# Float32 attention scores on 64 array rows per head for the first 14 head pairs, each loaded by fewer transfers

## The chip, the cores and the metric

One core of a Trainium2 chip runs the kernel. The metric is device time in microseconds of one execution, lower is better. Names of engines: PE is TensorE's matmul, PEld its weight load, DVE VectorE, ACT ScalarE, POOL GpSimd, SP the engine that issues most transfers.

## The reference

```python
batch, n_heads, seq, head_dim = (8, 12, 448, 64)

def _attn_ref(q, k, v):
    S = q.shape[2]
    scale = 1.0 / np.sqrt(q.shape[-1])
    scores = scale * np.matmul(q, k.transpose(0, 1, 3, 2)) - np.log(S)
    attn = 1.0 / (1.0 + np.exp(-scores))
    return np.matmul(attn, v).astype(np.float32)

def _moe_ref(x, w_in, w_out):          # x (3584, 768), w_in (768, 2048), w_out (2048, 768)
    h = x @ w_in
    beta = 1.0
    neg = h <= -beta
    pos = h >= beta
    g = np.where(pos, h, np.where(neg, 0.0, (h + beta) ** 2 / (4.0 * beta)))
    return (g @ w_out).astype(np.float32)
```

Attention weights are sigmoids, not a softmax. The attention output of all heads is laid out as 3584 tokens by 768 and goes through the feed-forward part. All inputs are float32; the weights come as 64-bit words whose two halves the kernel turns into float32 itself.

## The kernel before

*Pairs and pieces.* Two heads of 64 dimensions make one pair, so a batch has 6 pairs (`NP`) and there are 48 in all. A pair is worked in four pieces of keys (`NPC`): three of 128 keys and one "half piece" of the last 64, whose two heads share one tile. For each piece PE computes the scores of both heads (`scores`, tile `psc`, two buffers), ACT the sigmoid (`weigh`, lines 387 and 390), and PE multiplies it with v (`av`, line 436, tile `pav`). After the last piece the result is copied to `x32` (line 442 or 445). Pieces are counted through: piece 4p + c is the piece c of pair p.

*Three ways to compute scores.* Pairs 0 to 5 (`NFULL`) stay in float32. Their k is loaded twice over, each head's half beside zeros, so that a matmul over all 128 rows gives one head (line 339):

```python
out = psc[j * D : (j + 1) * D, 0, :S] if mid else psc[:, j, :S]
nc.tensor.matmul(out, r[:, 2 + j, w], r[:, 0, :], start=True, stop=True)
```

Pairs 6 to 13 (`NHALF`) have q and k scaled and split into a high and a low float16 part: the largest value by DVE (`prep_a`, line 275), a sum over partitions by PE (line 129), scales (line 106 on) and the split by ACT and DVE (`prep_b`, lines 310 and 311), then eight small transfers on SP that place the parts for stacked matmuls (lines 320 and 321, tile `qk`). A full piece is then two matmuls on 128 rows (line 346) and two on 64 rows (line 355), one per head each. Their v and attention weights stay float32. Pairs 14 to 47 split v and the weights too (lines 341, 361, 403, 404).

*Feed-forward.* The weights come in 16 chunks of 768 KB each for w_in and w_out. A chunk is loaded (line 166), converted by ACT (line 185) and DVE (lines 194, 195), its maximum taken (line 209, or 211 on ACT for w_out), and, once eight chunks have given a common scale, split to two float16 parts (lines 228, 229). `finish_x` scales and splits a batch's `x32` into `xhl` (lines 465, 466). `up` gives `ph` (line 534, 18 matmuls a chunk) and the activation `g` (lines 543 to 547), `down` gives `po` (line 566). The tiles `ph`, `po` and those of the small maxima share three buffers.

*Order of the work.* `step(i)` puts in the scores that run ahead and the `av` of piece i, and at given pieces the loads and preparations of later pairs. While batch b goes through `up` and `down`, the attention of batch b + 1 is dealt out between their units. The loads on SP keep program order in the opening; so does PE from batch 2 on. Everything else in batches 0 and 1 (PE, ACT, DVE, and SP later) is ordered by a list scheduler that plans with its own estimates of time, so an edit to one step can move others. Each engine then works through its list in that order, and waits where an operand isn't there yet. In the opening the loads of pairs 0 to 7 and of w_in are issued interleaved:

```python
load_pair(0)
wi.load(1, nc.sync)
load_pair(1)
wi.load(2, nc.sync)
load_pair(2)
wi.load(3, nc.sync)
```

and each conversion of a w_in chunk issues the load of a later one into the place that it freed (line 201).

Of the kernel before, what the change touches and what calls it, by code (L numbers as in the profile page):

```python
# [23 lines left out]
P = 128  # L24
# [9 lines left out]

NFULL = 6
NHALF = 8

# [11 lines left out]
L0 = 10  # L49
A0 = 17  # L50
LSTEP = 1
# [5 lines left out]
def sigmoid_attention_mlp(ctx: ExitStack, tc: tile.TileContext, first_qvk, qkv, w_in, w_out, out_t):  # L57
    nc = tc.nc
    NFULL, _, _, S = first_qvk.shape
    B = out_t.shape[1] // S  # L60
# [188 lines left out]
    def load_pair(p):  # L249
        if p >= NPAIR or not first_time("load", p):  # L250
            return
        if p < NFULL:
            r = full[:, p % NFB]
            nc.sync.dma_start(out=r[:D, 2, :], in_=first_qvk[p, :D, 2, :])
            nc.sync.dma_start(out=r[D:, 3, :], in_=first_qvk[p, D:, 2, :])
            nc.sync.dma_start(out=r[:, 0:2, :], in_=first_qvk[p, :, 0:2, :])
            ready[p] = r, r[:, 1]
            return
        src = qkv[p - NFULL]
        raws[p] = raw_p.tile([P, 2 * S + VW], F32, tag="raw", name="raw")  # L260
        if p < NFULL + NHALF:
            v = stk_p.tile([P, VW], F32, tag="v", name="v", bufs=3)
            nc.sync.dma_start(out=raws[p][:, : 2 * S], in_=src[:, : 2 * S])
            nc.sync.dma_start(out=v, in_=src[:, 2 * S :])
            ready[p] = v
        else:
            nc.sync.dma_start(out=raws[p], in_=src)

    def prep_a(p, total=True):
        if NFULL <= p < NPAIR and first_time("max", p):  # L270
            n = 2 if p < NFULL + NHALF else 3
            m = sml_p.tile([P, 3], F32, tag="m3", name="m3", bufs=2)
            parts = [(m[:, 0:2], raws[p][:, : 2 * S].rearrange("p (t n) -> p t n", t=2)), (m[:, 2:3], raws[p][:, 2 * S :])]
            for mt, rt in parts[: n - 1]:
# [13 lines left out]
    def prep_b(p):  # L288
        if not NFULL <= p < NPAIR or not first_time("split", p):
            return  # L290
        add_up(p)
        r, m = raws.pop(p), maxes.pop(p)[1]
        n = 2 if p < NFULL + NHALF else 3

# [5 lines left out]
        hl = stk_p.tile([P, 2, 2, S], F16, tag="hl", name="hl")  # L300
        parts = [hl[:, 0], hl[:, 1]]
        if n == 3:
            v = stk_p.tile([P, 2, VW], F16, tag="v", name="v", bufs=3)
            parts.append(v)
        else:
            v = ready[p]
        for t, dst in enumerate(parts):
# [18 lines left out]
    def scores(todo):  # L326

        tiles = []
        for i in todo:
            p, c = divmod(i, NPC)  # L330
            mid = c == NKC
            w = slice(c * P, S if mid else (c + 1) * P)
            psc = ps_sc.tile([P, 2, 512], F32, tag="psc", name="psc")
            tiles.append(psc)
            if p < NFULL:
                r = ready[p][0]
                for j in range(2):
                    out = psc[j * D : (j + 1) * D, 0, :S] if mid else psc[:, j, :S]
                    nc.tensor.matmul(out, r[:, 2 + j, w], r[:, 0, :], start=True, stop=True)  # L339
            elif mid and p >= NFULL + NHALF:  # L340
                nc.tensor.matmul(psc[:, 0, :S], corner(p), ready[p][4][:, 0, 1, :], start=True, stop=False)
            else:
                kq = ready[p][0]
                for j in range(2):
                    out = psc[j * D : (j + 1) * D, 0, :S] if mid else psc[:, j, :S]
                    nc.tensor.matmul(out, kq[:, j, 1, w], kq[:, j, 0, :], start=True, stop=False)  # L346
        for i, psc in zip(todo, tiles):
            p, c = divmod(i, NPC)
            mid = c == NKC
            if p >= NFULL and not (mid and p >= NFULL + NHALF):  # L350
                hl, w = ready[p][4], slice(c * P, S if mid else (c + 1) * P)
                for j in range(2):
                    rows = slice(j * D, (j + 1) * D)
                    out = psc[rows, 0, :S] if mid else psc[:, j, :S]
                    nc.tensor.matmul(out, hl[rows, 1, 0, w], hl[rows, 0, 1, :], start=False, stop=True)  # L355
        for i, psc in zip(todo, tiles):
            p, c = divmod(i, NPC)
            if p >= NFULL + NHALF and c == NKC:
                kq = ready[p][0]
# [6 lines left out]
        for p, c in (divmod(i, NPC) for i in todo):  # L366
            if c == 0 and p >= NFULL + NHALF:
                if p < NFULL + NHALF + 2:
                    nc.gpsimd.memset(corner(p), 0.0)
# [8 lines left out]
    def weigh(i, psc):  # L378
# [4 lines left out]
        a = psc[:, :n, :S]  # L383
        sqk = 1.0 / math.sqrt(D) if p < NFULL else ready[p][2]
        if p < NFULL + NHALF:
            a32 = att_p.tile([P, 2, S], F32, tag="ahl", name="a32")
# [22 lines left out]
    def av(i):  # L409
# [9 lines left out]
        v = ready[p][1]  # L419
        split = p >= NFULL + NHALF  # L420
        terms = []
        for j in range(2):
            o = slice(j * D, (j + 1) * D)
            full_v = slice((2 * c + j) * D, (2 * c + j + 1) * D)
            if p < NFULL and mid:
                full_v = slice(2 * c * D, (2 * c + 1) * D)
# [13 lines left out]
        if mid:  # L440
            if p < NFULL + NHALF:
                nc.scalar.activation(x32[:, hp, :], pav[:, :S], AF.Copy)
# [186 lines left out]
    with tc.manual_schedule(engines={mybir.EngineType.SP}):  # L629
# [9 lines left out]
        while at < NPIECE:  # L639
            step(at)  # L640
            at += 1
            for what, when in ((load_pair, L0), (prep_a, A0), (prep_b, A0 + 1)):
                for k in range(2):
                    if at == when + LSTEP * k:
                        what(NFULL + k)
            convert(wi, min((NA + 1) * at // WI_A, NA + 1 + max(0, at - WI_A) * (NFC - NA) // (NPIECE - WI_A + WI_B)))
# [110 lines left out]
```

## Time and profile before

| | us |
|---|---|
| median of 3 runs | 1175.96 |
| lowest and highest | 1175.06, 1177.38 |
| the profiled execution | 1175.71 |
| its span, first to last instruction | 1174.0 |

The span is what the trace covers; the rest of an execution's time lies around it. The page gives for each engine its busy time, which for PE is near to the span; busy PE can still be PE at work on matmuls that are slower than they need be, so the timeline's steps from one start to the next say more than the durations. A float32 matmul leaves two records in the trace, a float16 matmul one. In the timeline the numbers behind a tile's name are the array's rows and columns that the matmul uses. PEclk is the granted clock, where 1.00 is 2.4 GHz and 0.50 is 1.2 GHz.

### The profile page before, as it was taken

Reading aid. Unit: us, or ns where it says so; the run is one execution under the profiler, and the core shown is the slowest. Engines: PE = TensorE matmul, PEld = TensorE weight load, DVE = VectorE, ACT = ScalarE, POOL = GpSimd, SP = SyncE. Lnnn points to the kernel's source line nnn. Section 1 sums busy time; section 2 is a strip of 40 time slices with the busy share of each in tenths; the row PEclk is TensorE's granted clock in tenths of the full one; section 3 lists DMA queues with packets and bytes.
Section 4 is the critical chain, followed back from the end, with each engine's and each line's share of the span. In section 5 each row is a group of like instructions: output and inputs, shape, how many; then the busy total and the mean of one; then the engine's idle time right before and its main releaser. Section 6 shows DMA issues by size and latency. Waiting matters only on the chain.

```text
span 1174.0 us, 16804 instructions
## 1 busy us (share of the span) xinstructions
PE 1154.9 (98%) x6368; PEld 556.7 (47%) x6368; DVE 792.9 (68%) x1576; ACT 620.3 (53%) x897; POOL 30.5 (3%) x76
## 2 busy tenths in 40 slices
PE   7999999999999999999999999999999999999998
PEld 2334444454455444554455445454444544455554
DVE  6899986867644886578864887568865788326510
ACT  5788875644433665456643775446563557404300
POOL 0000000000000000000000000000000000000000
PEclk9989999999999999999999999999999999999999
DMA  9758352142112113111212221212123111000000
GB/s 328 276 183 287 104 166 93 43 134 65 49 56 65 41 41 97 57 56 44 78 58 65 59 72 49 72 54 77 41 60 94 56 42 25 24 25 8 1 16 32
DMA packets 49233, 93.71 MB, mean 80 GB/s; under 512 B 7936, under 2 KB 37888, under 8 KB 49152
## 3 DMA queue, kind: packets, MB, share of 16 engines
q1 hardware_dynamic: 47424, 83.20, 22.8%
q10 hardware_dynamic: 1728, 9.44, 2.3%
q8 instruction: 50, 0.82, 0.3%
q14 instruction: 31, 0.25, 0.1%
HBM read 60.95 MB, written 12.39 MB: 62 GB/s over the span
## 4 chain that ended last, share of the span: by engine, by line
PE 66%; DVE 17%; ACT 7%; DMA 7%; issue 2%; SPq 1%; ACTq 0%; DVEq 0%
PE po L566 37%; PE ph L534 16%; PE pav L436 6%; DMA raw<-qkv 5%; PE psc L346 3%; DVE g L545 2%; PE psc L339 2%; DVE m L275 2%; DVE g L544 2%; PE psc L355 2%; DVE ahl L404 2%; DVE ghl L547 2%; ACT psc L390 2%; ACT ghl L546 1%; DVE xhl L466 1%
## 5 line engine op out<-in xcount | busy, mean ns | idle before, releaser
L534 PE MATMUL ph<-xhl,w_in_sb 128*128 128x448 f16 x2304 | 448.7, 354 | 5.6 <-ACT xhl L465 2.7
L566 PE MATMUL po<-ghl,w_out_sb 128*128 128x448 f16 x2304 | 444.2, 353 | 0.0
L534 PEld LDWEIGHTS <-w_in_sb 128*128 128x128 f16 x2304 | 222.2, 98 | 225.0 <-issue 25.2
L566 PEld LDWEIGHTS <-w_out_sb 128*128 128x128 f16 x2304 | 222.0, 98 | 217.7 <-issue 13.4
L390 ACT ACTIVATE psc<-psc,nls,sqk 128x896 f32<-128x896 f32 (+1 forms) x136 | 126.8, 967 | 94.2 <-PE psc L355 93.3
L404 DVE SCALAR_TENSOR_TENSOR ahl<-psc,ahl 128x896 f16<-128x896 f32 x102 | 109.0, 1084 | 36.0 <-ACT ahl L403 35.7
L546 ACT ACTIVATE ghl<-g 128x448 f16<-128x448 f32 x128 | 73.6, 575 | 112.8 <-DVE g L545 111.4
L547 DVE TENSOR_TENSOR ghl<-g,ghl 128x448 f16<-128x448 f32 x128 | 79.6, 622 | 51.1 <-ACT ghl L546 50.9
L543 ACT ACTIVATE g<-ph,hr,ihr 128x448 f32<-128x448 f32 x128 | 91.7, 723 | 34.6 <-PE ph L534 30.1
L275 DVE TENSOR_REDUCE m<-raw 128x2 f32<-128x896 f32 x76 | 66.1, 902 | 53.5 <-DMA raw<-qkv 53.3
L576 DVE TENSOR_SCALAR o<-po,od 128x448 f32<-128x448 f32 x48 | 32.6, 681 | 90.9 <-PE po L566 82.0
L403 ACT ACTIVATE ahl<-psc 128x896 f16<-128x896 f32 x102 | 90.2, 913 | 0.0
L545 DVE SCALAR_TENSOR_TENSOR g<-ph,ihs,g 128x448 f32<-128x448 f32 x128 | 86.9, 681 | 2.5
L310 ACT ACTIVATE hl<-raw,qkv_s 128x448 f16<-128x448 f32 x84 | 51.7, 663 | 66.8 <-DVE qkv_i L112 50.7
L544 DVE SCALAR_TENSOR_TENSOR g<-g,rk 128x448 f32<-128x448 f32 x112 | 75.9, 680 | 15.2 <-ACT g L543 13.1
L346 PE MATMUL psc<-qk 128*128 128x448 f16 (+1 forms) x268 | 67.0, 354 | 1.7 <-DMA qk<-hl 1.6
L465 ACT ACTIVATE xhl<-x,x_s 128x448 f16<-128x448 f32 x48 | 27.7, 659 | 77.4 <-DVE x_s L108 77.4
L436 PE MATMUL pav<-ahl,v 128*64 128x448 f16 x612 | 64.2, 353 | 0.0
L311 DVE SCALAR_TENSOR_TENSOR hl<-raw,qkv_s,hl 128x448 f16<-128x448 f32 x84 | 54.8, 680 | 7.7 <-ACT hl L310 7.1
L436 PEld LDWEIGHTS <-v 128*64 128x64 f16 x748 | 42.3, 110 | 26.5 <-issue 0.9
L372 POOL COPY w_in_sb<-hl 64x64 f16<-64x64 f16 x68 | 29.4, 432 | 831.7 <-ACT hl L310 811.0
L339 PE MATMUL psc<-ghl 128*128 128x448 f32 (+1 forms) x96 | 39.2, 587 | 6.1 <-DMA ghl<-first_qvk 5.9
(109 smaller groups left out, 783.9 us busy)
## 6 DMA issues: line engine op xcount, KB each, us to landing
raw<-qkv SPq DMA_DIRECT2D x34, 704.0 KB, 4.4
qk<-hl SPq DMA_DIRECT2D x336, 56.0 KB, 2.0
w_out_sb<-w_in SPq DMA_DIRECT2D x16, 768.0 KB, 9.8
out_t<-o SPq DMA_DIRECT2D x48, 224.0 KB, 1.9
w_out_sb<-w_out ACTq DMA_DIRECT2D x6, 768.0 KB, 4.6
raww<-w_out ACTq DMA_DIRECT2D x6, 768.0 KB, 6.0
raw<-qkv SPq DMA_DIRECT2D x8, 448.0 KB, 6.2
w_out_sb<-w_out SPq DMA_DIRECT2D x4, 768.0 KB, 8.4
```

The lines of the kernel that those rows point to most:

```text
L275: nc.vector.tensor_reduce(out=mt, in_=rt, axis=AX.X, op=ALU.max, apply_absolute_value=True)
L346: nc.tensor.matmul(out, kq[:, j, 1, w], kq[:, j, 0, :], start=True, stop=False)
L390: nc.scalar.activation(a, a, AF.Sigmoid, bias=nls, scale=sqk)
L403: nc.scalar.activation(hi, x, AF.Copy, scale=ATT)
L404: nc.vector.scalar_tensor_tensor(out=lo, in0=x, scalar=ATT, in1=hi, op0=ALU.mult, op1=ALU.subtract)
L436: nc.tensor.matmul(pav[j * D : (j + 1) * D, :S], *terms[j][t], start=c == 0 and t == 0, stop=mid and t == len(terms[j]) - 1,)
L534: nc.tensor.matmul(ph[:, :S], w_in_sb[:, f, wh, c * P : (c + 1) * P], xhl[:, c, xh, :], start=c == 0 and wh + xh == 0, stop=c == NCC - 1 a ...
L543: nc.scalar.activation(g, ph[:, :S], AF.Relu, bias=hr, scale=ihr)
L544: nc.vector.scalar_tensor_tensor(out=g, in0=g, scalar=rt, in1=g, op0=ALU.min, op1=ALU.mult)
L545: nc.vector.scalar_tensor_tensor(out=g, in0=ph[:, :S], scalar=ihs, in1=g, op0=ALU.mult, op1=ALU.max)
L547: (nc.gpsimd if f % GPOOL else nc.vector).tensor_tensor(out=ghl[:, f, 1, :], in0=g, in1=hi, op=ALU.subtract)
L566: nc.tensor.matmul(po[:, :S], w_out_sb[:, f, wh, m * P : (m + 1) * P], ghl[:, f, gh, :], start=f == lo and wh + gh == 0, stop=f == hi - 1 ...
```

## The change

Pairs 0 to 13 (`NF32`) now take one path. Scores are one float32 matmul per head on the 64 rows that hold the head's q and k: head 0 on rows 0 to 63, head 1 on rows 64 to 127, with both heads issued one after the other. k is no longer doubled and no zeros are set. For pairs 0 to 5 (`NFIRST`) q, k and v lie side by side in memory and come in one transfer (pair 0: q and k, then v), into five buffers instead of four. Pairs 6 to 13 keep their two transfers, but their q and k are used as loaded: the maximum, the sum, the split and the eight small transfers are gone for them. Pairs from 14 on are as before. The order in which `load_pair` and `wi.load` are called is as before.

```diff
-NFULL = 6
-NHALF = 8
+NFIRST = 6
+NF32 = 14
...
-    NFB = 4
-    full = ghl.rearrange("p f h n -> p (f h n)").bitcast(F32).rearrange("p (b t n) -> p b t n", b=NFB, t=4)
-    for i in range(NFB):
-        nc.vector.memset(full[D:, i, 2, :], 0.0)
-        nc.vector.memset(full[:D, i, 3, :], 0.0)
+    NFB = 5
+    full = ghl.rearrange("p f h n -> p (f h n)")[:, : NFB * 6 * S].bitcast(F32)
+    full = full.rearrange("p (b t n) -> p b t n", b=NFB, t=3)
...
-        if p < NFULL:
+        if p < NFIRST:
             r = full[:, p % NFB]
-            nc.sync.dma_start(out=r[:D, 2, :], in_=first_qvk[p, :D, 2, :])
-            nc.sync.dma_start(out=r[D:, 3, :], in_=first_qvk[p, D:, 2, :])
-            nc.sync.dma_start(out=r[:, 0:2, :], in_=first_qvk[p, :, 0:2, :])
-            ready[p] = r, r[:, 1]
+            for t in (slice(0, 2), slice(2, 3)) if p == 0 else (slice(0, 3),):
+                nc.sync.dma_start(out=r[:, t, :], in_=first_qvk[p, :, t, :])
+            ready[p] = (r[:, 0], r[:, 1]), r[:, 2]
             return
...
-        if p < NFULL + NHALF:
+        raw = raw_p.tile([P, 2 * S + VW], F32, tag="raw", name="raw")
+        if p < NF32:
             v = stk_p.tile([P, VW], F32, tag="v", name="v", bufs=3)
-            nc.sync.dma_start(out=raws[p][:, : 2 * S], in_=src[:, : 2 * S])
+            nc.sync.dma_start(out=raw[:, : 2 * S], in_=src[:, : 2 * S])
             nc.sync.dma_start(out=v, in_=src[:, 2 * S :])
-            ready[p] = v
+            ready[p] = (raw[:, :S], raw[:, S : 2 * S]), v
...
-            if p < NFULL:
-                r = ready[p][0]
+            if p < NF32:
+                q, k = ready[p][0]
                 for j in range(2):
-                    out = psc[j * D : (j + 1) * D, 0, :S] if mid else psc[:, j, :S]
-                    nc.tensor.matmul(out, r[:, 2 + j, w], r[:, 0, :], start=True, stop=True)
+                    rows = slice(j * D, (j + 1) * D)
+                    out = psc[rows, 0, :S] if mid else psc[:, j, :S]
+                    nc.tensor.matmul(out, k[rows, w], q[rows, :], start=True, stop=True)
```

Elsewhere `NFULL + NHALF` becomes `NF32`, the preparations of the split run from pair 14 on only, and the host packs q, k, v of pairs 0 to 5 in this order.

The scheduler deals the work out anew. Two places:

ACT in the opening, before: conversions of w_in chunks 7 to 10 (line 185) among the sigmoids (line 387, `a` is the sigmoid's tile), in full, piece 10 to 15, and the first split (line 228).

```order
L387 ACTIVATE a_220<-psc,nls 128x896 [waits PE_49,Activation_49]
L387 ACTIVATE a_237<-psc,nls 128x448 [waits PE_49,Activation_49]
L185 ACTIVATE w_in_sb<-w_out_sb 128x768 [waits DMAHW6_49]
L185 ACTIVATE w_in_sb<-w_out_sb 128x768 [waits DMAHW7_49]
L387 ACTIVATE a_245<-psc,nls 128x896 [waits PE_49,Activation_49]
L185 ACTIVATE w_in_sb<-w_out_sb 128x768 [waits DMAHW0_49]
L387 ACTIVATE a_261<-psc,nls 128x896 [waits PE_49,Activation_49]
L442 ACTIVATE x_91<-pav 128x448 [waits PE_49]
L387 ACTIVATE a_277<-psc,nls 128x896 [waits PE_49,Activation_49]
L387 ACTIVATE a_286<-psc,nls 128x448 [waits PE_49,Activation_49]
L185 ACTIVATE w_in_sb<-w_out_sb 128x768 [waits DMAHW6_49]
L228 ACTIVATE w_in_sb<-w_in_sb,wi_s 128x768 [waits DVE_49]
```

ACT now, the same four conversions (now line 184): they stand among pieces 6 to 9 (line 379).

```order
L434 ACTIVATE x_91<-pav 128x448 [waits PE_49]
L184 ACTIVATE w_in_sb<-w_out_sb 128x768 [waits DMAHW5_49]
L379 ACTIVATE a_157<-psc,nls 128x896 [waits PE_49,Activation_49]
L184 ACTIVATE w_in_sb<-w_out_sb 128x768 [waits DMAHW6_49]
L379 ACTIVATE a_171<-psc,nls 128x448 [waits PE_49,Activation_49]
L184 ACTIVATE w_in_sb<-w_out_sb 128x768 [waits DMAHW7_49]
L379 ACTIVATE a_184<-psc,nls 128x896 [waits PE_49,Activation_49]
L379 ACTIVATE a_191<-psc,nls 128x896 [waits PE_49,Activation_49]
L184 ACTIVATE w_in_sb<-w_out_sb 128x768 [waits DMAHW3_49]
L434 ACTIVATE x_91<-pav 128x448 [waits PE_49]
L227 ACTIVATE w_in_sb<-w_in_sb,wi_s 128x768 [waits DVE_49]
L379 ACTIVATE a_203<-psc,nls 128x896 [waits PE_49,Activation_49]
```

Chunk 10's conversion stood behind the sigmoids of 16 pieces and now stands behind those of 10; chunks 2 to 15 all moved up in this way against the sigmoids.

PE while the attention of batch 1 runs among the feed-forward of batch 0, before: the third piece of pair 11, its four matmuls in one row.

```order
L346 MATMUL psc_1479<-qk_1222 128x448 [waits Activation_49]
L346 LDWEIGHTS qk_1222
L346 MATMUL psc_1479<-qk_1222 128x448
L355 LDWEIGHTS hl_1217
L355 MATMUL psc_1479<-hl_1217 128x448
L355 LDWEIGHTS hl_1217
L355 MATMUL psc_1479<-hl_1217 128x448
L566 LDWEIGHTS w_out_sb_90 [waits DVE_49]
```

PE now, the same piece (line 333), between `po` matmuls (line 558):

```order
L558 LDWEIGHTS w_out_sb_90
L558 MATMUL po_1183<-ghl_93,w_out_sb_90 128x448
L333 MATMUL psc_1213<-raw_791 128x448 [waits PE_49]
L558 LDWEIGHTS w_out_sb_90 [waits DVE_49]
L558 MATMUL po_1183<-ghl_93,w_out_sb_90 128x448
L333 MATMUL psc_1213<-raw_791 128x448
L558 LDWEIGHTS w_out_sb_90 [waits Activation_49]
```

The two heads' matmuls of this piece now have a `po` matmul between them. In the whole list this is so for four score pieces: three full ones (the first of pairs 8 and 12, and this one) and the half piece of pair 11. The `pav` pairs that are torn in this way are two now and were four before.

## Rows read from the trace of the kernel before

**Rows 1.** The page: its first line, and PE's part of its first section.
```profile
span 1174.0 us, 16804 instructions
PE 1154.9 (98%) x6368; PEld 556.7 (47%) x6368; DVE 792.9 (68%) x1576; ACT 620.3 (53%) x897; POOL 30.5 (3%) x76
```

**Rows 2.** PE's list of waits: who waited for whom, us in total, times, longest us.
```profile
PE ph L534 <- ACT xhl L465: 2.7, 1, 2.7
PE psc L346 <- DMA qk<-hl: 1.6, 3, 1.0
```

**Rows 3.** PE's timeline, opening: start us, us, engine, line, operation, records, idle before.
```profile
27.51 1.77 PE L339 MATMUL psc<-ghl 128*128 128x448 f32 x4
29.21 0.97 PE L436 MATMUL pav<-a,ghl 64*64 64x448 f32 x4
30.11 2.67 PE L339 MATMUL psc<-ghl 128*128 128x448 f32 x8
32.61 1.67 PE L436 MATMUL pav<-a,ghl 128*64 128x448 f32 x8
34.22 1.77 PE L339 MATMUL psc<-ghl 128*128 128x448 f32 x4
```

**Rows 4.** PE's timeline, pairs 5 to 7 and the first `ph`.
```profile
62.25 0.55 PE L346 MATMUL psc<-qk 128*128 128x448 f16 x2
62.73 0.36 PE L355 MATMUL psc<-hl 64*128 64x448 f16 x2
63.02 0.97 PE L436 MATMUL pav<-a,ghl 128*64 128x448 f32 x4
...
64.71 0.97 PE L436 MATMUL pav<-a,ghl 64*64 64x448 f32 x4
65.61 0.55 PE L346 MATMUL psc<-qk 128*128 128x448 f16 x2
...
66.39 0.38 PE L346 MATMUL psc<-qk 128*64 128x448 f16 x2
...
67.00 1.72 PE L436 MATMUL pav<-a,v 128*64 128x448 f32 x8
...
76.25 0.53 PE L534 MATMUL ph<-xhl,w_in_sb 128*128 128x448 f16 x1 [2.71 <-ACT xhl L465]
...
76.65 12.80 PE L534 MATMUL ph<-xhl,w_in_sb 128*128 128x448 f16 x53
```

**Rows 5.** Windows: busy of PE, PEld, DVE, ACT, POOL; PEclk, DMA share, GB/s.
```profile
15.00:20.00 5.00, 5.00 (x18) 1.65 (x16) 3.94 (x6) 3.21 (x4) 0.00 (x0) 1.00 1.02 418
2.60:41.30 38.70, 35.23 (x111) 12.87 (x113) 26.90 (x40) 23.44 (x29) 0.00 (x0) 1.00 1.02 367
75.40:82.00 6.60, 5.75 (x17) 2.39 (x17) 6.60 (x18) 6.45 (x12) 0.00 (x0) 0.50 0.15 60
```

**Rows 6.** SP's timeline, then the list of DMA issues (KB, us to landing): w_in chunk 10.
```profile
31.61 0.36 SPq L166 DMA_DIRECT2D w_out_sb<-w_in  x1
...
w_out_sb<-w_in SPq DMA_DIRECT2D x1, 768.0 KB, 9.7
```

**Rows 7.** ACT's timeline from the end of pair 3's third full piece on.
```profile
48.05 1.01 ACT L387 ACTIVATE a<-psc,nls 128x896 f32<-128x896 f32 x1 [1.59 <-PE psc L339]
48.96 0.54 ACT L442 ACTIVATE x<-pav 128x448 f32<-128x448 f32 x1
49.38 0.90 ACT L185 ACTIVATE w_in_sb<-w_out_sb 128x768 f32<-128x768 f32 x1
50.17 0.94 ACT L228 ACTIVATE w_in_sb<-w_in_sb,wi_s 128x768 f16<-128x768 f32 x1
51.00 1.54 ACT L387 ACTIVATE a<-psc,nls 128x896 f32<-128x896 f32 x2
```

**Rows 8.** PE's timeline, later: one head of `pav` alone.
```profile
162.33 0.96 PE L436 MATMUL pav<-a,v 64*64 64x448 f32 x2
163.22 0.55 PE L346 MATMUL psc<-qk 128*128 128x448 f16 x2
```

More of the change, by code (lines that the diff above doesn't have):

```diff
@@ L49 @@
 L0 = 10
-A0 = 17
 LSTEP = 1
@@ L288, in prep_b @@
     def prep_b(p):
-        if not NFULL <= p < NPAIR or not first_time("split", p):
+        if not NF32 <= p < NPAIR or not first_time("split", p):
             return
@@ L300, in prep_b @@
         hl = stk_p.tile([P, 2, 2, S], F16, tag="hl", name="hl")
[L301 to L306, printed above, removed]
+        v = stk_p.tile([P, 2, VW], F16, tag="v", name="v", bufs=3)
+        parts = [hl[:, 0], hl[:, 1], v]
         for t, dst in enumerate(parts):
@@ L344, in scores @@
                 for j in range(2):
-                    out = psc[j * D : (j + 1) * D, 0, :S] if mid else psc[:, j, :S]
-                    nc.tensor.matmul(out, kq[:, j, 1, w], kq[:, j, 0, :], start=True, stop=False)
+                    nc.tensor.matmul(psc[:, j, :S], kq[:, j, 1, w], kq[:, j, 0, :], start=True, stop=False)
         for i, psc in zip(todo, tiles):
@@ L349, in scores @@
             mid = c == NKC
-            if p >= NFULL and not (mid and p >= NFULL + NHALF):
-                hl, w = ready[p][4], slice(c * P, S if mid else (c + 1) * P)
+            if p >= NF32 and not mid:
+                hl, w = ready[p][4], slice(c * P, (c + 1) * P)
                 for j in range(2):
                     rows = slice(j * D, (j + 1) * D)
-                    out = psc[rows, 0, :S] if mid else psc[:, j, :S]
-                    nc.tensor.matmul(out, hl[rows, 1, 0, w], hl[rows, 0, 1, :], start=False, stop=True)
+                    nc.tensor.matmul(psc[:, j, :S], hl[rows, 1, 0, w], hl[rows, 0, 1, :], start=False, stop=True)
         for i, psc in zip(todo, tiles):
             p, c = divmod(i, NPC)
-            if p >= NFULL + NHALF and c == NKC:
+            if p >= NF32 and c == NKC:
                 kq = ready[p][0]
@@ L366, in scores @@
         for p, c in (divmod(i, NPC) for i in todo):
-            if c == 0 and p >= NFULL + NHALF:
-                if p < NFULL + NHALF + 2:
+            if c == 0 and p >= NF32:
+                if p < NF32 + 2:
                     nc.gpsimd.memset(corner(p), 0.0)
@@ L419, in av @@
         v = ready[p][1]
-        split = p >= NFULL + NHALF
+        split = p >= NF32
         terms = []
@@ L424, in av @@
             full_v = slice((2 * c + j) * D, (2 * c + j + 1) * D)
-            if p < NFULL and mid:
+            if p < NFIRST and mid:
                 full_v = slice(2 * c * D, (2 * c + 1) * D)
@@ L589, in step @@
         p, c = divmod(i, NPC)
-        early = p >= NFULL + NHALF
+        early = p >= NF32
         if c == 0:
@@ L596, in step @@
                 prep_a(p + 2)
-        if c == 1 and p >= NFULL + NHALF - 1:
+        if c == 1 and p >= NF32 - 1:
             prep_a(p + 3, False)
@@ L600, in step @@
             prep_b(p + 2)
-        if c == 3 and p >= NFULL + NHALF - 2:
+        if c == 3 and p >= NF32 - 2:
             load_pair(p + 4)
         if not early:
-            more, some = i + LAG + 1 + (p == NFULL + NHALF - 1 and c == NKC), [i]
+            more, some = i + LAG + 1 + (p == NF32 - 1 and c == NKC), [i]
         else:
@@ L641, in sigmoid_attention_mlp @@
             at += 1
[L642 to L645, printed above, removed]
+            for k in range(2):
+                if at == L0 + LSTEP * k:
+                    load_pair(NFIRST + k)
             convert(wi, min((NA + 1) * at // WI_A, NA + 1 + max(0, at - WI_A) * (NFC - NA) // (NPIECE - WI_A + WI_B)))
@@ L739 @@
     half = vp[:, :, NK * P :]
-    n = NFULL
-    first = np.stack([qt[:n], np.concatenate([whole[:n], half[:n].reshape(n, P, D)], 2), kt[:n]], 2)
+    n = NFIRST
+    first = np.stack([qt[:n], kt[:n], np.concatenate([whole[:n], half[:n].reshape(n, P, D)], 2)], 2)
     half = half[n:].transpose(0, 2, 1, 3).reshape(B * NP - n, P // 2, P)
```

24 lines of the change are left out of this document (12 added, 12 removed).

## Prediction

> **What bounds the kernel now.** I read the page first. PE is busy 1154.9 of 1174.0 us [rows 1], so a change pays only if it takes work off PE or closes one of PE's few gaps. The list of PE's waits names those gaps in the part that changes: 2.7 us in one piece before the first `ph`, which waits for `xhl`, and 1.6 us in three pieces where scores wait for the small loads of `qk` [rows 2].
>
> Then PE's timeline of the opening, where pairs 0 to 5 run in float32 [rows 3]. A piece is up to 128 keys of one pair, with both heads; each pair has three full pieces and one half piece (keys 384 to 447). A float32 matmul leaves two records. From start to start, the scores of a full piece take 1.70 us (27.51 to 29.21), because the two heads use all 128 rows one after the other. The two heads of `pav` share the array by columns and take 0.90 us. A full and a half piece together take 2.50 us, so the half piece, whose heads lie side by side, takes 0.80; two `pav` in a row take 1.61.
>
> Rows 4 show pairs 6 and 7, which use split float16. A full piece takes 0.77 us (62.25 to 63.02) and a half piece 0.61 (66.39 to 67.00). The last `pav` of batch 0 ends at 65.61 and the first `ph` starts at 76.25. I call the first of these T. After the gap the granted clock stands at 0.50, that is 1.2 GHz, from 75.4 to 82.0 us; PE is busy 5.75 us of that stretch [rows 5] and half of it, 2.9 us, is lost.
>
> Last, the loads. From 2.6 to 41.3 us the 16 DMA engines are fully busy and move 367 GB/s; in a stretch where most of what moves is weights it is 418 [rows 5]. The eleventh w_in chunk (number 10) is issued at 31.61 and lands 9.7 us later, at 41.3 [rows 6].
>
> **The change, part by part.**
>
> *Scores of pairs 0 to 5.* Eighteen full pieces lose one of their two passes over the array. The trace has no float32 matmul on 64 rows by 128 columns. Nearest is the float32 pair on 64 rows by 64 columns, 0.90 us for both heads (64.71 to 65.61) [rows 4]; the lower bound is the half piece's 0.80, the upper the 1.70 of two heads in turn [rows 3]. I take 0.88. In float16 the form 64 by 128 is there: both heads take 0.29 us (62.73 to 63.02) [rows 4], against 0.48 for the two full-array matmuls before them, so they do overlap. With `pav` a pair then costs 3 x 0.88 + 0.80 + 3.4 = 6.8 us, 1.71 a piece, where it cost 9.31 (1.70 + 0.90 + 2.50 + 1.61 + 1.70 + 0.90). PE saves some 13 us in the opening.
>
> A rule speaks against the half pieces, whose two heads write one PSUM bank. The Trainium skill, TensorEngine Tiling (Array Packing), Restrictions and Gotchas, says that different row tiles cannot access the same bank at once. By that rule each half piece would take about 1.7 us, not 0.88. The trace does not bear it out: the `pav` half pieces on 64 by 64 write one bank with both heads and take 0.90.
>
> *Does the saving reach T?* I think not, and this is the centre of the forecast. ACT works in order, and the scheduler has placed the w_in conversions much earlier: chunk 10 now stands after ten sigmoids, before it stood after sixteen. But chunk 10 comes behind the same 13.5 MB (eleven chunks of 0.79 MB, pairs 0 to 6), and the engines are already full. The pair loads become one block of 5.4 KB a row instead of rows of 1.8 and 3.6 KB; if pairs move at 418 instead of some 335 GB/s, six pairs of 0.69 MB gain 2.4 us. So chunk 10 lands at about 38.9 (bounds 36.4, everything at 418, and 41.3, as now), and ACT holds the next sigmoid, PE the next scores, until then. PE idles some 5 us.
>
> From there I count ACT by start-to-start times [rows 7]: conversion 0.79, `x` copy 0.42, split 0.83, sigmoid 0.91 gives 41.85. Up to the sigmoid of piece 16 stand four full sigmoids and two half ones (0.50), five conversions (chunks 11 to 15), four splits and one copy: 3.6 + 1.0 + 4.0 + 3.3 + 0.4 = 12.3 us, ending at 54.2. PE needs 6 x 1.71 = 10.3 for the same pieces, so ACT sets the pace, and PE has 2.0 us of slack. A gap of 2.7 us was enough to halve the clock [rows 2, 5]; after a gap of 5 I charge 2.9 again, of which 0.9 is not covered. Then PE sets the pace with 8 scores and 8 `pav`, 13.7 us. T = 54.2 + 13.7 + 0.9 = 68.8, which is 3.2 us **later** than the 65.6 of before.
>
> *From T to the first `ph`.* The order has four scores and four `pav` there, 6.85 us: `ph` starts at 75.65. The chain to `xhl` fits in this (copy, maximum, transpose, scales, first xhl, some 5 us when DVE is not holding pair preparation), so the 2.7 us wait and the slow clock after it go. Before, two more score pieces were done by then: 1.75 us. Front: (75.65 + 1.75) - (76.25 + 2.9) = **-1.75**, bounds -4.2 and +0.6 from the landing.
>
> *Scores of pairs 8 to 13, beside the feed-forward work.* PE is full here, so work counts fully. A pair cost 3 x 0.77 + 0.61 = 2.92; it now costs 4 x 0.88 = 3.5. Six pairs: **+3.5**, bounds +1.7 (0.80 a piece) and +5.2 (0.95).
>
> *Torn pieces.* In the new PE order four score pieces have `ph` or `po` matmuls between their heads. A lone float32 head takes 0.89 (162.33 to 163.22) [rows 8], as much as a pair. Torn scores add 4 x 0.85; torn `pav` pairs fall from four to two. Net **+1.7**.
>
> *What is dropped.* Eight maxima, sixteen splits on ACT and on DVE, 64 small `qk` loads on SP, eight fills of zeros on DVE at the start. Of all this PE waits only for the `qk` loads: **-1.6** [rows 2]. The rest is freed time on engines that PE doesn't wait for.
>
> *What is added in waits.* Raw q and k now stay in use until the scores have read them. On SP the load of pair 8 waits for the scores of pair 6, at T + 1.7, and w_out chunks 0 and 1 are queued behind it. Chunk 2 waits behind the load of v of pair 9, which waits for pair 6's last `pav` (75.65). ACT converts these in order, ahead of the `g` that frees `ph`'s buffers: with some 7 us for chunk 2's load (9.7 in a full stretch [rows 6]) and two more operations, the first `g` comes at about 85. PE needs the buffer after three `ph` and two pieces, some 13 us after its start, at 89 (53 `ph` matmuls took 12.8 us at mostly half clock [rows 4]; I take 10 for 54). The margin is thin, so I charge **+1.5**, between 0 and 5, a little over the 4.3 us of waits that PE has there now [rows 2].
>
> *Sum.* -1.75 + 3.5 + 1.7 - 1.6 + 1.5 = +3.35. The profiled execution took 1175.71 us, 0.25 under the median of the runs, 1175.96. That gives **1179.0 us**.
>
> **Rivals.**
>
> 1. *ACT is not held, and the opening runs at PE's new pace.* PE would need only 1.71 us a piece, ACT some 42 us in all (18 x 0.91 + 6 x 0.50 + 16 x 0.79 + 9 x 0.83 + 6 x 0.42). If the chunks landed early enough for T = 60, the front would gain 8.8 more: 1170. It decides at T = 65.4, where the sum is zero. For it: DVE drops the pair preparation, and SP issues fewer and larger loads. Against it: even for 65.4 chunk 10 would have to land at 35.5, that is 13.5 MB in 33 us, 410 GB/s for everything, against 367 in the same stretch now [rows 5]. Chance 0.22.
> 2. *No change that can be measured.* The landing at its early bound, a piece at 0.82, no new wait: 3.35 - 2.5 - 1.4 - 1.5, a little faster; any one of them alone gives 1176.5 to 1178. Chance 0.27.
> 3. *The heads do not overlap.* Full pieces alone: eleven on the way to `ph` that ACT doesn't cover and fifteen later that aren't torn anyway, times 0.82, 21 us: 1200. Against it stand the pairs at 0.29 and 0.90 [rows 4]. If the heads of the half pieces took turns, the twelve on the way or later would cost 0.85 more each, 10 us: 1189. The rule of the Trainium skill, TensorEngine Tiling (Array Packing), that is cited above would have it so; the 0.90 speaks against it. Chance of either 0.05.
> 4. *A longer hold of ACT by w_out loads*: each load that ACT awaits with a score's sigmoid behind it costs up to 5 us; 1182 to 1188. It is in the upper part of my range.
>
> **How the numbers follow.** The smallest change a measurement of this kernel tells is about 0.2%, 2.35 us. The forecast and rival 4 hold 0.46, rival 3 has 0.05: slower 0.51. Rival 2: 0.27. Rival 1: 0.22. The likeliest case alone spans 1175 to 1188. The range of 8 in 10 goes down to rival 1's 1170, and up to 1188, where late landing (+2.4), 0.95 a piece (+1.7) and 5 us of waits (+3.5) together give 1186.6.
>
> **What would show it.** Scores of a full piece in the opening near 0.88 from start to start, both heads starting together; 1.7 would be rival 3. ACT waiting for w_in loads between 20 and 40 us where now it waits for PE; a PE gap of 4 to 5 us ended by a sigmoid near 41; a second stretch at half clock there. T between 66 and 71, `ph` starting at 73 to 78 with no wait for `xhl`. No wait of scores for `qk`. After 82 us, a little more score time and four torn pieces. If T is below 64, the centre of this forecast is wrong; if T is right but the end is not, the terms after `ph` are.

## The result and the profile after

The changed kernel takes **1184.24 us** (median of 4 runs, 1183.12 to 1185.78), the kernel before, beside it, 1176.63. The ratio of the runs is 1.0071, with a 95% interval of 1.0056 to 1.0087: slower. The medians differ by 7.6 us (their own quotient is 1.0065). The forecast was 1179, slower, with 1170 to 1188. The profiled execution of the changed kernel is the longest of its four, 1185.78 us, 10.1 above that of before; the accounts below are between these two executions.

The page's first lines stand against [rows 1]: PE is as busy as before in a span that is 10.1 us longer, so PE has lost time to waiting: it is idle in 29.6 us of the span, before in 19.1. Within its busy time a gain and a loss cancel: the scores of the opening got cheaper and later ones dearer, so that all score matmuls together take 148.3 us from start to start, before 149.3.

```profile
span 1184.1 us, 16533 instructions
PE 1154.5 (97%) x6360; PEld 548.6 (46%) x6360; DVE 769.9 (65%) x1496; ACT 609.8 (51%) x881; POOL 30.2 (3%) x76
```

PE's list of waits, changed kernel (who waited for whom, us in all, times, longest). Both entries of [rows 2] are gone, and a new one heads the list: scores (line 333) that wait for the sigmoid (line 379) to free their buffer, which was 0.2 us before.

```profile
PE psc L333 <- ACT a L379: 13.1, 7, 5.1
PE psc L333 <- DMA ghl<-first_qvk: 4.1, 1, 4.1
PE pav L428 <- ACT x L434: 3.6, 4, 2.2
PE ph L526 <- DVE g L537: 3.2, 5, 1.5
PE psc L335 <- DVE ahl L396: 1.6, 4, 0.5
```

PE's timeline of the opening. A full piece's scores take 0.95 us from start to start (18.64 to 19.59), where [rows 3] had 1.70: the heads do overlap. But PE stands still three times in the opening, 5.14, 4.06 and 2.19 us. The last `pav` of batch 0 ends at 70.59 (before: 65.6), the first `ph` starts at 77.96 (before: 76.25), without a wait for xhl and at full clock.

```profile
12.59 1.86 PE L333 MATMUL psc<-ghl 64*128 64x448 f32 x4 [5.14 <-ACT a L379]
...
18.64 1.02 PE L333 MATMUL psc<-ghl 64*128 64x448 f32 x4
19.59 0.97 PE L428 MATMUL pav<-a,ghl 128*64 128x448 f32 x4
...
27.43 1.34 PE L333 MATMUL psc<-ghl 64*64 64x448 f32 x4 [4.06 <-ACT a L379]
...
39.60 1.72 PE L428 MATMUL pav<-a,ghl 128*64 128x448 f32 x8 [2.19 <-ACT x L434]
...
69.69 0.97 PE L428 MATMUL pav<-a,ghl 64*64 64x448 f32 x4
70.59 1.92 PE L333 MATMUL psc<-raw 64*128 64x448 f32 x8
...
77.96 10.39 PE L526 MATMUL ph<-xhl,w_in_sb 128*128 128x448 f16 x54
```

ACT's timeline tells what each sigmoid stood behind: w_in conversions (line 184) that wait for their loads. The row at 38.23 is chunk 10, which had its place behind ten pieces' sigmoids. The three stops of PE end right behind the rows at 9.33 (with the table load and the sigmoid after it), 25.58 and 38.23.

```profile
9.33 0.89 ACT L184 ACTIVATE w_in_sb<-w_out_sb 128x768 f32<-128x768 f32 x1 [7.25 <-DMA w_out_sb<-w_in]
...
25.58 0.89 ACT L184 ACTIVATE w_in_sb<-w_out_sb 128x768 f32<-128x768 f32 x1 [2.61 <-DMA w_out_sb<-w_in]
26.38 0.99 ACT L379 ACTIVATE a<-psc,nls 128x896 f32<-128x896 f32 x1
...
29.10 0.90 ACT L184 ACTIVATE w_in_sb<-w_out_sb 128x768 f32<-128x768 f32 x1 [1.29 <-DMA w_out_sb<-w_in]
...
38.23 0.89 ACT L184 ACTIVATE w_in_sb<-w_out_sb 128x768 f32<-128x768 f32 x1 [2.61 <-DMA w_out_sb<-w_in]
39.02 0.53 ACT L434 ACTIVATE x<-pav 128x448 f32<-128x448 f32 x1
```

Later, a torn score piece between `po` matmuls (PE's timeline): each head takes 0.95 us (168.34 to 169.29) by itself, as long as both side by side.

```profile
168.34 1.02 PE L333 MATMUL psc<-raw 64*128 64x448 f32 x2
169.29 0.36 PE L558 MATMUL po<-ghl,w_out_sb 128*128 128x448 f16 x1
169.59 1.02 PE L333 MATMUL psc<-raw 64*128 64x448 f32 x2
170.53 0.55 PE L558 MATMUL po<-ghl,w_out_sb 128*128 128x448 f16 x2
```

### The profile page after: what moved, and what is told of

It reads as the page before. It is cut to its first block, busy times and chain, and to the rows that moved or that the text cites. A ratio compares the mean times of both kernels' runs of the same rounds, so it can differ in the third digit from the quotient of the medians.

```text
span 1184.1 us, 16533 instructions
## 1 busy us (share of the span) xinstructions
PE 1154.5 (97%) x6360; PEld 548.6 (46%) x6360; DVE 769.9 (65%) x1496; ACT 609.8 (51%) x881; POOL 30.2 (3%) x76
## 4 chain that ended last, share of the span: by engine, by line
PE 67%; DVE 15%; DMA 9%; ACT 8%; issue 1%; SPq 0%; ACTq 0%; DVEq 0%
PE po L558 37%; PE ph L526 18%; PE pav L428 6%; DMA raw<-qkv 4%; DMA w_out_sb<-w_in 3%; PE psc L339 2%; DVE g L537 2%; PE psc L333 2%; DVE m L272 2%; DVE g L536 2%; DMA w_out_sb<-w_out 2%; DVE ahl L396 2%; DVE ghl L539 2%; PE psc L347 1%; ACT psc L382 1%; ACT ghl L538 1%
## 5 line engine op out<-in xcount | busy, mean ns | idle before, releaser
L272 DVE TENSOR_REDUCE m<-raw 128x2 f32<-128x896 f32 x68 | 57.6, 881 | 52.0 <-DMA raw<-qkv 52.0
L303 ACT ACTIVATE hl<-raw,qkv_s 128x448 f16<-128x448 f32 x68 | 41.8, 663 | 64.9 <-DVE qkv_i L111 52.6
L379 ACT ACTIVATE a<-psc,nls 128x896 f32<-128x896 f32 (+1 forms) x56 | 49.9, 905 | 21.1 <-PE psc L333 21.1
L339 PE MATMUL psc<-qk 128*128 128x448 f16 x204 | 50.1, 352 | 0.0
L304 DVE SCALAR_TENSOR_TENSOR hl<-raw,qkv_s,hl 128x448 f16<-128x448 f32 x68 | 44.5, 680 | 6.5 <-ACT hl L303 6.4
```

## The experiments

**Theory A**: two separate losses. Before the first `ph`, ACT's list puts conversions whose loads are still under way ahead of sigmoids whose scores are done; later, lone heads cost as much as pairs. Each kernel was timed against the kernel before on its own chip, which took 1174.8 to 1175.0 there, so kernels are compared by these ratios. With 1.0071 the changed kernel would take some 1183 there.

*1. ACT in program order.*

```diff
-                nc.scalar.activation(
+                act = nc.scalar.activation(
                     a, self.words_of(f)[1].bitcast(F32), AF.Prelu, scale=HIGH_SCALE, alpha=SIGN_SLOPE
                 )
+                if self is wi:
+                    tc.keep_in_program_order(act)
```

The added call keeps an instruction behind the one that the program writes directly before it on the same engine. The scheduler deals the rest out anew around it: up to the changed kernel's first `ph`, PE's order stays the same but for the small `pm` matmuls, DVE's does not.

> Edit: on ACT the w_in conversions of the changed kernel stay behind the sigmoids and copies that the program writes before them; nothing else is touched. Theory A (in the opening PE is held by ACT's order: a conversion that waits for its load stands ahead of sigmoids whose scores are done): PE's waits for sigmoids before the first ph fall from 15.7 us to under 6, the last pav of batch 0 or the first ph comes 6 to 12 us earlier, and the run takes 1174 to 1179 us. Rival B (ACT's and DVE's amount of work, or the loads themselves, hold the opening whatever the order): the waits turn up under another name, the first ph comes no earlier, 1183 to 1187 us. Rival C (the gain is there at the first ph and is lost again behind it, in waits for w_in chunks or for g): an earlier ph, but 1181 to 1185 us.

Measured: 1177.50 us, ratio 1.0020 (1.0011 to 1.0029), about 6 us less than the changed kernel. The last `pav` of batch 0 ends at 61.7 instead of 70.6, and the first `ph` comes at 71.98 instead of 77.96 (PE's timeline):

```profile
60.77 0.97 PE L430 MATMUL pav<-a,v 64*64 64x448 f32 x4
...
65.75 1.76 PE L335 MATMUL psc<-raw 64*64 64x448 f32 x4 [2.90 <-ACT a L381]
68.47 3.22 PE L335 MATMUL psc<-raw 64*128 64x448 f32 x8 [0.96 <-ACT a L381]
71.98 0.73 PE L528 MATMUL ph<-xhl,w_in_sb 128*128 128x448 f16 x3 [0.29 <-ACT xhl L459]
```

PE is busy in all of 10 to 45 us. Two windows of that stretch (columns as in [rows 5]), then ACT's waits between 4 and 80 us, which turn round: it waits for scores and no longer for w_in.

```profile
30.00:35.00 5.00, 5.00 (x26) 1.47 (x24) 4.90 (x8) 4.11 (x7) 0.00 (x0) 1.00 1.02 413
35.00:40.00 5.00, 5.00 (x23) 1.29 (x23) 4.72 (x9) 4.49 (x6) 0.00 (x0) 1.00 1.03 413
```

```profile
ACT a L381 <- PE psc L335: 11.5, 11, 3.9
ACT w_out_sb L184 <- DMA w_out_sb<-w_out: 2.5, 1, 2.5
```

B falls: loads and amounts of work were as before, and 9 us of the opening came back with the order alone. PE's waits for sigmoids before the first `ph` are 4.9 us, under the 6 that A asked for; in the changed kernel they are 11.6 (the 15.7 of the expectation takes in the 4.1 us for the first load). Of the 4.9, 3.9 come after 61.7 us (2.90 and 0.96), where a w_out conversion that waited 2.5 us for its load stood ahead of a sigmoid. So C is true of a part: of the 9 us, 6 are left at the first `ph`.

*2. and 3. The two halves of the change apart.* The first kernel is that of before with the change's `load_pair` and `scores` for `p < 6` alone. The second is the changed kernel with the loads, zero fills and scores of before for pairs 0 to 5. The scores' part of each diff:

```diff
             if p < NFULL:
-                r = ready[p][0]
+                q, k = ready[p][0]
                 for j in range(2):
-                    out = psc[j * D : (j + 1) * D, 0, :S] if mid else psc[:, j, :S]
-                    nc.tensor.matmul(out, r[:, 2 + j, w], r[:, 0, :], start=True, stop=True)
+                    rows = slice(j * D, (j + 1) * D)
+                    out = psc[rows, 0, :S] if mid else psc[:, j, :S]
+                    nc.tensor.matmul(out, k[rows, w], q[rows, :], start=True, stop=True)
```

```diff
-                q, k = ready[p][0]
+                if p < NFIRST:
+                    r = ready[p][0]
+                    for j in range(2):
+                        out = psc[j * D : (j + 1) * D, 0, :S] if mid else psc[:, j, :S]
+                        nc.tensor.matmul(out, r[:, 2 + j, w], r[:, 0, :], start=True, stop=True)
+                    continue
+                q, k = ready[p][0]
```

> Edit: the kernel before, with 64-row float32 scores and one load for pairs 0 to 5 alone; pairs 6 to 13 keep their split float16 scores, their preparation and their small qk loads. Theory A: the saving of pairs 0 to 5 on PE (0.75 us for each of 18 full pieces) is mostly eaten by ACT's order, and nothing is lost after the first ph, so the run stands 1 to 4 us on the fast side of the kernel before: 1172 to 1176 us. Rival D (the opening alone makes the changed kernel slower): 1181 to 1185 us. Rival E (the opening would gain its whole 9 us, and pairs 6 to 13 take it away): 1166 to 1169 us.

> Edit: the complement. Pairs 0 to 5 as in the kernel before (scores on all 128 rows with zeros, three loads a pair, their zero fills); pairs 6 to 13 with 64-row float32 scores from the raw tiles, as in the changed kernel. Theory A: scores of these pairs beside full PE cost 0.13 us a piece more, four torn pieces 0.9 each, new waits 2 to 3.6 us, no qk waits (-1.6): 1180 to 1184 us. Rival D (the loss is in the opening): 1175 to 1178 us.

Measured: pairs 0 to 5 alone 1185.18 us, ratio 1.0082 (1.0069 to 1.0096); pairs 6 to 13 alone 1182.50, ratio 1.0061 (1.0049 to 1.0074). The second came as expected. The first did not: I had counted on 1172 to 1176, and the half of the change that saves PE some 13 us is by itself as slow as the whole. That is near the time of D, but D also asked for 1175 to 1178 from the other half, which took 1182.50; E falls. PE waits 14.6 us for sigmoids before its first `ph`. The trace shows where: the small `qk` loads of pairs 6 and 7 are still there, and SP issues them ahead of the last w_in chunk. First SP's timeline, then ACT's, of this kernel:

```profile
58.84 0.59 SPq L318 DMA_DIRECT2D qk<-hl  x1
59.47 0.58 SPq L166 DMA_DIRECT2D w_out_sb<-w_in  x1
```

```profile
64.22 0.89 ACT L185 ACTIVATE w_in_sb<-w_out_sb 128x768 f32<-128x768 f32 x1 [1.89 <-DMA w_out_sb<-w_in]
65.00 1.00 ACT L385 ACTIVATE a<-psc,nls 128x896 f32<-128x896 f32 x1
```

Sixteen `qk` loads take SP from 45.8 to 59.4; a sigmoid stands behind that chunk's conversion, and w_out conversions behind late loads stand before xhl. The first `ph` starts only at 86.68. The halves' losses, 0.82% and 0.61%, don't add up to the whole's 0.71%; the change of pairs 6 to 13, for one, takes away the `qk` loads that stand in the way here. No run changes the loads of pairs 0 to 5 without their scores, so what the loads alone do is not shown.

*4. Whole pieces.* The second head directly follows the first on PE, for scores and float32 `pav`. The scores' part of the diff; that of `pav` is of the same kind.

```diff
-                    nc.tensor.matmul(out, k[rows, w], q[rows, :], start=True, stop=True)
+                    with tc.high_priority(offset=400 * j):
+                        mm = nc.tensor.matmul(out, k[rows, w], q[rows, :], start=True, stop=True)
+                    if j:
+                        tc.keep_in_program_order(mm)
```

> Edit: in the changed kernel the second head of each float32 score piece and of each float32 pav directly follows the first on PE, so the torn pieces between 95 and 245 us are whole; the rest of the order stays. Theory A (a lone head takes as long as both side by side, some 0.95 us): four scores and two pav pieces become whole, 3.5 to 5 us are gained, 1179 to 1181 us. Rival F (a lone head overlaps with the feed-forward matmuls around it, or the wait behind which it was torn comes back on PE): under 1 us, 1183 to 1185 us.

Measured: 1178.27 us, ratio 1.0030 (1.0019 to 1.0041), about 4.8 us less than the changed kernel; F falls. PE's timeline, the same piece as above: both heads in 0.95 us (166.35 to 167.30).

```profile
166.35 1.02 PE L334 MATMUL psc<-raw 64*128 64x448 f32 x4
167.30 0.74 PE L564 MATMUL po<-ghl,w_out_sb 128*128 128x448 f16 x3
```

Added up from start to start, from the first `ph` to the run of 36 `ph` at 237.0 us (243.9 in the changed kernel), float32 scores take 24.5 us and `pav` 25.1; in the changed kernel 28.3 and 26.8. That is 3.8 us for four torn score pieces and 1.6 for two torn `pav`. (`pav` had four torn pieces in the kernel before, so not all of this is a loss by the change.)

*5. and 6. Pairs of edits.* `whole_in_order` joins edits 1 and 4; `next_eight_whole` joins edits 3 and 4.

> Edit: the changed kernel with both edits at once: w_in conversions behind the sigmoids on ACT (act_in_order, 1177.5 us) and every score piece and pav whole (pieces_whole, 1178.3 us). Theory A (two separate losses, ACT's order before the first ph and lone heads after it): the gains add up, 1171 to 1174 us, below the kernel before. Rival F (both edits remove the same idle time): 1176 to 1178 us.

> Edit: next_eight_only (1182.5 us) with every 64-row score piece and float32 pav whole. Theory A: the lone heads (0.95 us each, four scores and two pav pieces) go, 3.5 to 5 us: 1177 to 1179.5 us; what is left over the kernel before, 3 us, is the 0.13 us a piece for 24 pieces less the qk waits, and new waits. Rival F: 1181 to 1183 us.

Measured: 1171.35 us, ratio 0.9969 (0.9956 to 0.9981), and 1177.25 us, ratio 1.0011 (0.9999 to 1.0022). The gains of edits 1 and 4 add up: 0.51% and 0.41% alone, 1.02% together. The two losses are separate, and the change without them is faster than the kernel before. In the second kernel whole pieces give back 0.50%; three score pieces and three `pav` had been torn there, not four and two.

*7. and 8. Is program order on ACT good in itself?* Edit 1 put on `first_six_only`, and on the kernel before:

> Edit: first_six_only (1185.2 us) with the w_in conversions behind the sigmoids on ACT. In first_six_only PE waited 12.9 us for sigmoids and 4.3 us for xhl, and w_in chunk 15 was issued on SP only at 59.5 us, behind 16 small qk loads. Theory A (ACT's order is the hold): PE's waits for sigmoids before the first ph fall under 4 us and the run takes 1169 to 1176 us. Rival G (the qk loads on SP hold the last w_in chunk, and through it xhl, whatever ACT's order is): PE still waits 4 us or more for xhl, the first ph comes after 80 us, 1179 to 1185 us.

> Control: the kernel before with the same edit on ACT (w_in conversions behind the sigmoids), nothing else. Theory A: before the change PE, not ACT, set the pace of the opening (a full piece's scores take 1.70 us there), so the order of ACT held nothing and the edit gains nothing there: 1172 to 1178 us, against 5 to 7 us gained in the changed kernel. Rival J (the edit is good for either kernel, and says nothing on why the changed one is slower): 1167 to 1171 us.

Measured: 1175.94 us, ratio 1.0004 (0.9992 to 1.0016), and **1187.34 us, ratio 1.0105** (1.0087 to 1.0122). The first is at the far end of what A said: PE waits 4.1 us for sigmoids before the first `ph`, just over the 4 that A allowed. The first `ph` comes at 71.4, 15 us earlier than in `first_six_only`, but PE still waits 5.1 us for xhl, and of G that much is true. The second is a miss for A and for J, which looked for no effect or a gain. Here scores take 1.70 us, PE is late, and ACT in program order waits for PE instead of converting what has landed. ACT's waits for scores up to 90 us, first in the kernel before and then with the edit, and the first entry of PE's list with the edit:

```profile
ACT a L387 <- PE psc L339: 10.2, 11, 1.7
```

```profile
ACT a L389 <- PE psc L341: 24.4, 16, 7.1
```

```profile
PE ph L536 <- ACT xhl L467: 6.9, 2, 4.7
```

ACT stands 24.4 us, and the conversions and splits that it could have done then come late, among the last sigmoids and ahead of xhl; the first `ph` comes at 81.36, where it was 76.25. So in these kernels neither order is right by itself: the early conversions are good where PE is the slower one, and program order where PE is fast.

*9. and 10. The gap before the first `ph`.* In `whole_in_order` 10 us pass between the last `pav` of batch 0 (60.8) and the first `ph` (70.8), and PE does four score pieces in them, 3.8 us. `xhl_first` binds w_out's first four conversions as edit 1 binds those of w_in; `casts_first` binds them to the last xhl cast. The two diffs, each against `whole_in_order`:

```diff
-                if self is wi:
+                if self is wi or f < 4:
                     tc.keep_in_program_order(act)
```

```diff
+                last = state.get("cast")
+                with tc.issue_after(last.ins) if self is wo and f < 4 else nullcontext():
...
-            nc.scalar.activation(xhl[:, hp, 0, :], x32[:, hp, :], AF.Copy, scale=s)
+            state["cast"] = nc.scalar.activation(xhl[:, hp, 0, :], x32[:, hp, :], AF.Copy, scale=s)
```

> Edit: whole_in_order, with the first four w_out conversions on ACT behind what the program writes before them (so behind the six xhl casts) instead of ahead of them. In act_in_order the last pav of batch 0 ended at 61.7 us and the first ph came only at 72.0: a w_out conversion that waited 2.5 us for its load, two more and their sums stood ahead of two sigmoids and of xhl. Theory A: the first ph comes at 67 to 70 us, and the run takes 2 to 4 us less than whole_in_order. Rival H (the chain of small DVE operations from the last x to the scales sets the time of xhl, not ACT's order; or the later w_out conversions hold g behind the first ph): no gain, or up to 3 us slower than whole_in_order.

> Edit: whole_in_order, with the first four w_out conversions on ACT put behind the last of the six xhl casts outright. In xhl_first they stood only behind the instruction written directly before each, so two of them still came ahead of xhl (63.4 and 65.3 us, the first waiting 2.0 us for its load) and the first ph came at 71.3, not at the 67 to 70 that was expected. Theory A: with none ahead, PE's waits of 2.4 and 1.8 us for sigmoids before the first ph go, the first ph comes at 66 to 69 us, 1165 to 1169 us. Rival H (DVE's chain to the scales sets xhl): the first ph stays at 70 to 72 us, 1168 to 1171 us.

Measured: 1169.65 us, ratio 0.9947 (0.9930 to 0.9964), with the first `ph` at 71.29, not at 67 to 70. The edit did not do what I had said: a conversion was bound to the instruction written directly before it, not to xhl, and two still came ahead. `casts_first`: **1166.08 us, ratio 0.9916** (0.9901 to 0.9932), the first `ph` at 67.62, as A expected; H falls. PE's timeline of `casts_first`:

```profile
60.29 0.97 PE L436 MATMUL pav<-a,v 64*64 64x448 f32 x4
...
62.31 0.97 PE L338 MATMUL psc<-raw 64*64 64x448 f32 x4
65.56 2.13 PE L338 MATMUL psc<-raw 64*128 64x448 f32 x8 [2.29 <-ACT a L386]
67.62 11.72 PE L536 MATMUL ph<-xhl,w_in_sb 128*128 128x448 f16 x54
```

This is the fastest version, 0.84% under the kernel before. The 2.29 us that PE still waits at 65.56 are of the same kind: on ACT the sigmoids stand behind a w_in split (63.68) that waited 1.85 us for DVE.

*11. and 12. The loads of w_out.* Two edits of `casts_first`. `casts_first_early_w_out` loads w_out's first two chunks three conversions sooner; `w_out_before_pair_8` leaves them and moves pair 8's load behind the loop of the opening.

```diff
-            if w is wi and w.at in (NFC - 3, NFC + 1):
+            if w is wi and w.at in (NFC - 6, NFC + 1):
```

```diff
         if c == 0:
-            load_pair(p + 3)
+            if p + 3 != NFIRST + 2:
+                load_pair(p + 3)
...
+        load_pair(NFIRST + 2)
     with tc.high_priority(offset=X_PRIO):
         inv_x = finish_x(0)
```

> Edit: casts_first, with the loads of w_out chunks 0 and 1 written ahead of the load of pair 8 on SP, where they don't wait until the scores of pair 6 have left a raw tile. Theory A (the wait of that load on SP makes the w_out conversions late, and with them g and the sums behind the first ph): the first w_out load is issued 3 to 8 us earlier, ACT's waits for w_out loads go, up to 3 us gained. Rival I (with the conversions behind xhl the loads land in time anyway, or pair 8 comes later instead): within 1 us of casts_first.

> Edit: casts_first, with the load of pair 8 written after the loads of w_out chunks 0 and 1 and not before them; the order on PE, ACT and DVE stays the same to the row, only SP's changes. Theory A (SP waits to issue pair 8's load until the scores of pair 6 have left a raw tile, and the w_out loads behind it come late): the first w_out load is issued at 52 to 56 us instead of 57.9, ACT's wait of 1.1 us for it goes, and 0.5 to 2 us are gained: 1164 to 1165.5 us. Rival I (the loads land in time anyway, or pair 8 comes late in their place): 1165.5 to 1168 us.

Measured: 1170.71 us, ratio 0.9960 (0.9945 to 0.9976), and 1166.40 us, ratio 0.9919 (0.9905 to 0.9932). The first says nothing on the question: in it w_out chunks 0 and 1 land on the words of w_in chunks 10 and 11 before these are converted, so it converts other data, and the first of these two conversions waits 3.04 us for the new load. The second is clean. The first w_out load is issued at 48.43, where it was 57.92, and nothing is gained (ACT's wait for a w_out load near 80 us is still there, 1.45 us, in `casts_first` 1.08): I holds, and A's expectation here was wrong. SP's place for these loads is no cost once the conversions stand behind xhl. Whether it was one in the changed kernel, where the first is issued at 73.45, these two runs don't tell; it stays open.

## Why the prediction was right, and where not

It was right in its sign and its range, not in its size: +3.35 was forecast, the medians differ by 7.6 and the two profiled executions by 10.1. Every term but that of the `qk` loads came out dearer than it was put, and the measured time lies within 1170 to 1188 because that range was wide. Its main thought held: ACT works in order, conversions moved ahead of sigmoids hold them, so PE's saving doesn't reach the first `ph`. Experiments 1 and 5 show it. The Trainium skill, PSUM — Partial Sum Buffer, Engine vs sequencer instructions, says that ScalarE's queue is strictly first in, first out; the rows above agree: the sigmoid at 26.38 waited until the conversion of 25.58 was done, though the last scores before PE's stop had ended by 23.4. Term by term, for the two profiled executions:

- *Scores of pairs 0 to 5.* 0.88 a piece was taken; 0.95 was measured, 0.90 for a half piece. (The "some 13 us" saved on PE don't follow from the prediction's own terms: 9.31 less 6.84 a pair is 14.8 for six. With 0.95 and 0.90 it is 12.9.) The rule of the Trainium skill, TensorEngine Tiling (Array Packing), Restrictions and Gotchas, that different row tiles cannot access one PSUM bank at the same time, read as two heads that take turns, would have made each half piece last about 1.7 us; the trace does not agree. Rival 3 falls in both its forms. A half piece in PE's timeline of `casts_first`, at full clock, 54.93 to 55.83:

```profile
54.93 0.97 PE L338 MATMUL psc<-raw 64*64 64x448 f32 x4 [0.88 <-ACT a L386]
55.83 1.72 PE L436 MATMUL pav<-a,v 128*64 128x448 f32 x8
```

- *The front, -1.75.* Measured +0.7: `ph` starts at 77.96 with two score pieces more still to do (1.9), against 76.25 and 2.9 of slow clock. The hold on ACT came as counted: chunk 10's conversion was forecast for 38.9 and started at 38.23 (the 335 GB/s behind that forecast is not worked out from a row), and piece 16's sigmoid was forecast to end at 54.2 and ended at 53.9. PE's stops before 38 us change nothing in this count, because ACT works from 38.23 to 55 us without a pause of over 0.1 us and sets the pace. What failed is the step from there to T, 13.7 us for eight scores and eight `pav` and 0.9 of slow clock. The matmuls took 14.7, and PE stood 1.9 more behind sigmoids and an `x` copy that came late on ACT, because w_in splits (line 227) stood ahead of them, the first of which waited 1.69 us for DVE; the prediction counted no such wait. T was 70.6, not 68.8, and from T to `ph` it took 7.4, not 6.85. ACT's timeline, then PE's:

```profile
59.77 0.93 ACT L227 ACTIVATE w_in_sb<-w_in_sb,wi_s 128x768 f16<-128x768 f32 x1 [1.69 <-DVE w_in_sb L228]
60.61 0.99 ACT L379 ACTIVATE a<-psc,nls 128x896 f32<-128x896 f32 x1
```

```profile
61.65 1.02 PE L333 MATMUL psc<-ghl 64*128 64x448 f32 x4 [0.27 <-ACT a L379]
63.67 0.97 PE L333 MATMUL psc<-ghl 64*64 64x448 f32 x4 [1.00 <-ACT a L379]
65.23 1.72 PE L428 MATMUL pav<-a,ghl 128*64 128x448 f32 x8 [0.59 <-ACT x L434]
```

The wait for xhl and the slow clock behind it went, as said. The gap of 4 to 5 us near 41 was one of 2.19 at 39.6, and the half clock after it did not come: the clock stood at 1.00 from 35 to 45 us, and was low after the earlier gaps, as the windows of the changed kernel show (columns as in [rows 5]).

```profile
10.00:15.00 5.00, 2.41 (x6) 0.80 (x8) 3.19 (x5) 4.46 (x6) 0.00 (x0) 0.58 1.02 422
25.00:30.00 5.00, 2.57 (x8) 0.73 (x10) 4.54 (x6) 3.12 (x5) 0.00 (x0) 0.79 1.02 418
35.00:45.00 10.00, 7.81 (x37) 2.07 (x33) 8.97 (x17) 7.32 (x10) 0.00 (x0) 1.00 1.02 411
```

- *Scores of pairs 8 to 13, +3.5.* Measured +4.8: the 24 pieces take 22.6 us, 0.94 each, where they took 17.8 in the same stretch of before, 0.74 each. The 0.73 from [rows 4] was right and 0.88 too low; 0.95, the upper bound of this term, is what came.
- *Torn pieces, +1.7.* Mis-sized: +2.8. Four lone heads of scores cost 3.8 (forecast 3.4), and `pav` in this stretch fell by 1.0 (27.8 to 26.8), not by 1.7. Experiment 4 shows 5.4 us for all lone heads of the changed kernel.
- *qk waits, -1.6.* As said; the list of waits no longer has them.
- *New waits, +1.5.* Mis-sized: PE waits 3.6 us between the first `ph` and 250 us, and the `g` wait of 1.53 us at 93.70 is the one that was described.

These sum to +0.7 + 4.8 + 2.8 - 1.6 + 3.6 = +10.3, against 10.1 us between the two executions. What is left nearly cancels: up to 250 us `ph` and `po` take 1.9 more and the small `pm` 0.5 less, and PE's waits after that are 1.4 less.

*Rival 1* (ACT not held, T = 60, 1170) was given 0.22. `act_in_order` is that case made: T = 61.7, but 1177.5, because of the 9 us at T only 6 are left at the first `ph`; one for one was too high a price. (`casts_first`, with T = 61.2, took 1166.1, but with whole pieces and with w_out's conversions moved, which the rival did not have.) What spoke against it was read wrongly. I had asked for chunk 10 to land by 35.5, taking ACT's list as given. In `act_in_order` the loads move at 413 GB/s between 30 and 40 us, in the changed kernel at 411, and PE does not stop: nothing but a place in a list tied sigmoids to that landing.

## What to carry to other kernels

When an engine gets faster, read again the lists of those that feed and drain it: an order that suits a slow engine holds a fast one, and the other way round (edit 1 gained 0.5% in one kernel and cost 1.05% in the other). Look for an instruction that waits for a transfer and stands ahead of work whose inputs are there, and bind it behind that work by name, not to whatever is written before it. Two matmuls that share the array by rows paid here only where they were neighbours, so keep them together in the order.

## What was not expected of the hardware

A float32 matmul on 64 rows by 128 columns with 448 elements takes 0.95 us whether it runs alone or beside its twin on the other 64 rows; making all lone heads of scores and `pav` whole gave back 0.41 of the 0.71% (experiment 4). The granted clock fell after gaps of 5.14 and 4.06 us in the opening (0.58 and 0.79 over the 5 us windows that hold the restart), while a gap of 2.19 us at 39.6 left it at 1.00. In [rows 2, 5] a gap of 2.7 us was followed by 0.50.
